# The products of the spectra behind the next row maxima in VectorE's order

## The chip, the cores and the metric

The kernel runs on one core of one Trainium2 chip. The core has five engines that run side by side, each through its own list of instructions in order: TensorE (PE, matrix products; its weight loads are shown apart as PEld), VectorE (DVE), ScalarE (ACT), GpSimd (POOL) and SyncE (SP, which here issues transfers). TensorE writes its results into PSUM, a small memory that VectorE and ScalarE read. The metric is the time of one execution on the device, in microseconds (us).

## The reference

The input `A_u` (1 x 2048 x 448) goes through two branches, and a gate per row mixes their outputs. Branch a is a state-space layer: a convolution along the 2048 rows, by way of a Fourier transform, with a filter made from the parameters. Branch b is attention with a memory: 16 heads of width 28 over 4 segments of 512 rows.

```python
def _A_ref(u, ...):
    K = 2.0 * jnp.einsum("dn,dnl->dl", C, P).real
    Kf = jnp.fft.rfft(K, L2)
    Uf = jnp.fft.rfft(u_t, L2)
    y = jnp.fft.irfft(Uf * Kf[None, :, :], L2)[:, :, :L]
...
def _B_ref(x, wq, wk, wv, wo, beta):
    for s in range(N):
        logits = jnp.einsum("bhqd,bhkd->bhqk", qs, ks) * scale + mask
        p = _softmax(logits, axis=-1)
        a_dot = jnp.einsum("bhqk,bhkd->bhqd", p, vs)
        ...
        o = g * a_mem + (1.0 - g) * a_dot
...
return g * a + (1 - g) * b
```

The product `Uf * Kf` is what the change touches. The row maximum that the softmax subtracts is what it is ordered against.

## The kernel before

The program has two halves. The first (about 425 us) makes the filter, the projections of the attention and the first step of the transform of `u`. The second half, `second_half`, weaves three streams of work into one order that is written out by hand. It loops over 16 blocks `i` (four segments of four groups of heads), and in each over six rounds `r`. One round takes one step of each stream:

- `weigh(i)`: three batches of matmuls `ps_w<-qu,ku` (the logits) and then one exponential on ScalarE, `PT<-ps_w`.
- `maxima(i + 2)`, two blocks ahead: first matmuls that lay the causal mask into a PSUM tile (`ps_mx<-mk`, "the masks" below), then the logits on top (`ps_mx<-ku,qu`), then one or two reductions on VectorE, `mx<-ps_mx` (a round with two covers 384 and 128 columns). `pair` interleaves these with the three batches of `weigh`: batch, masks, batch, logits and reduction, batch.
- `values(i - 1)`, in the first three rounds of a block: matmuls `ps_pv<-PT,V`.
- pieces of the end of a segment (`seg_end`): matmuls into `ps_m`, each read by one VectorE instruction that rescales a tile (`pvs`, `am`) or makes an output row block (`tb`).
- one step of `convolve`, in blocks 1 to 12. It works through 16 units `m`, which I count 1 to 16 in order of time. Its steps are, a round each: `transform(m)` (matmuls `ps_c<-gk,cf`, a copy `ks<-ps_c` by ScalarE and two transfers that swap halves of `ks`); `product(m - 1)` (matmuls `ps_c<-gu,cf`, then two VectorE multiplications `pr<-ps_c,ks`, "the products" below); an empty step; and `back(m - 1)` (matmuls `ps_c<-pr,cb`, in one round or two, then a copy `bs<-ps_c`).

The PSUM tiles `ps_w`, `ps_mx`, `ps_c`, `ps_m` and `ps_pv` exist once each. So the masks of a round wait for the reduction of the round before, `back` waits for both products, and a matmul into `ps_m` waits for the VectorE instruction that reads the last contents.

VectorE's instructions of this half go through `k.dve`, and each is pinned behind the one issued before it: the order of the Python calls is VectorE's order. `product` is called at the end of a round, so its two multiplications stand ahead of the reduction of the next round. All records of helpers carry the line of the helper: L1453 for VectorE and ScalarE here, L1499 for matmuls, L1502 for transposes.

## Time and profile before

| | us |
|---|---|
| runs, in rising order | 793.38, 797.98, 798.75 |
| median of the runs | 797.98 |
| the profiled execution | 792.33 |
| its span, first to last instruction | 790.5 |

The profiled execution is a fourth one, and its rows are what the prediction reads. Its stage of interest runs from about 477 to 705 us after the span's start: the stretch with the convolution's units 1 to 16. A row of the timeline gives start and duration in us, the engine, the line, the operation, the tiles (`out<-in`) with their shapes and how many instructions were merged into the row; in brackets stands how long the engine had been idle and what ended that. A weight load and a matmul are separate rows.

### The profile page before, as it was taken

How to read it: one execution, taken by the hardware profiler on the slowest of the kernel's cores; microseconds unless marked ns; L12 is line 12 of the kernel's file. 1: busy time of each engine (PE TensorE's matmuls, PEld its weight loads, DVE VectorE, ACT ScalarE, POOL GpSimd, SP SyncE). 2: the span in 40 equal slices, each digit the busy share in tenths (PEclk: the TensorE clock that was granted, in tenths of full speed). 3: DMA queues.
4: the chain of work that ended last, by engine and by line, in shares of the span. 5: the costliest groups of instructions: out<-in, count | busy, mean ns of one | idle time of the engine just before them, and what ended most of it. 6: DMA issues, size and time to landing. Idle time of an engine off the chain costs nothing.

```text
span 790.5 us, 19759 instructions
## 1 busy us (share of the span) xinstructions
PE 680.0 (86%) x8262; PEld 371.9 (47%) x8278; DVE 572.7 (72%) x768; ACT 493.8 (62%) x611; POOL 157.6 (20%) x193
## 2 busy tenths in 40 slices
PE   1695998999888998889996799889998899879997
PEld 1362565666555665556653443333443333334333
DVE  8989579878998798897976645655545755583486
ACT  4867689889998899998984225555434623451120
POOL 5304300111011101111020012414111411141110
PEclk9998999999999999999999979998998989999699
DMA  9338674135562345633457888997766875565875
GB/s 249 116 86 249 211 242 140 59 107 184 160 186 103 107 145 162 221 119 102 155 194 283 309 322 235 379 319 232 242 240 217 289 247 163 179 208 218 216 241 161
DMA packets 91550, 158.00 MB, mean 200 GB/s; under 512 B 22174, under 2 KB 59542, under 8 KB 91462
## 3 DMA queue, kind: packets, MB, share of 16 engines
q1 hardware_dynamic: 85530, 153.55, 59.4%
q10 hardware_dynamic: 5052, 2.33, 1.2%
q8 instruction: 65, 1.06, 0.6%
q0 software_dynamic: 880, 0.87, 0.3%
q14 instruction: 23, 0.19, 0.1%
HBM read 88.51 MB, written 60.24 MB: 188 GB/s over the span
## 4 chain that ended last, share of the span: by engine, by line
PE 54%; ACT 18%; DVE 14%; DMA 6%; issue 5%; SPq 2%; ACTq 0%; POOL 0%; DVEq 0%
PE ps_m L1499 22%; PE ps_c L1499 9%; ACT cs L1453 6%; PE ps_w L1499 5%; PE ps_mx L1499 5%; PE ps_pv L1499 5%; PE ps_k L1499 4%; PE ps_arg L1499 4%; DVE mx L1453 2%; DVE pr L1453 2%; DMA ku<-KD 2%; ACT EY L1453 2%; ACT L1453 1%; PE ps_m L1502 1%; DVE Y L413 1%
## 5 line engine op out<-in xcount | busy, mean ns | idle before, releaser
L1453 ACT ACTIVATE PT<-ps_w 128x1024 f32<-128x1024 f32 (+1 forms) x96 | 84.6, 881 | 145.1 <-PE ps_w L1499 139.2
L1453 DVE TENSOR_REDUCE mx<-ps_mx 128x2 f32<-128x1024 f32 (+3 forms) x128 | 102.4, 821 | 86.0 <-PE ps_mx L1499 83.7
L366 POOL TENSOR_TENSOR EX<-EX,cab 128x1024 f32<-128x1024 f32 x28 | 53.5, 1914 | 291.4 <-ACT EX L1453 269.0
L1453 ACT ACTIVATE cs<-ps_arg 128x1024 f32<-128x1024 f32 x97 | 94.5, 1024 | 8.6 <-DVE cs L386 6.2
L1499 PE MATMUL ps_w<-qu,ku 32*128 32x512 f32 (+3 forms) x768 | 94.7, 360 | 4.1 <-ACT PT L1453 4.0
L1094 POOL TENSOR_SCALAR_AFFINE_SELECT PT<-PT 128x256 f32<-128x256 f32 (+1 forms) x96 | 47.8, 498 | 241.8 <-ACT PT L1453 241.7
L1499 PEld LDWEIGHTS ps_w<-qu,ku 32*128 32x128 f32 x768 | 60.8, 195 | 70.5 <-ACT PT L1453 35.4
L1499 PE MATMUL ps_m<-xh,w 112*128 112x512 f32 x256 | 91.6, 410 | 0.2 <-DMA w<-WD 0.2
L1499 PE MATMUL ps_k<-Y,X 128*32 128x64 f32 x3584 | 63.8, 225 | 15.5 <-DVE Y L414 15.5
L409 DVE TENSOR_TENSOR X<-EX,cs 128x1024 f32<-128x1024 f32 x56 | 70.2, 1254 | 8.1 <-ACT cs L1453 7.5
L1499 PEld LDWEIGHTS ps_k<-Y,X 128*32 128x32 f32 x3584 | 54.5, 113 | 40.5 <-DVE Y L414 24.7
L413 DVE TENSOR_TENSOR Y<-EY,cs 128x1024 f32<-128x1024 f32 x56 | 68.2, 1218 | 0.0
L1453 ACT ACTIVATE cs<-cs 128x1024 f32<-128x1024 f32 x56 | 59.3, 1058 | 1.3
L1499 PEld LDWEIGHTS ps_m<-xh,w 112*128 112x128 f32 x256 | 48.0, 188 | 20.9 <-issue 10.0
L1453 ACT ACTIVATE EY<-ps_arg 128x1024 f32<-128x1024 f32 x52 | 52.1, 1040 | 5.3 <-PE ps_arg L1499 5.1
L1499 PE MATMUL ps_mx<-mk 32*128 32x128 bf16 (+5 forms) x768 | 36.4, 215 | 19.0 <-DVE mx L1453 19.0
L1499 PE MATMUL ps_m<-xl,w 112*128 112x512 f32 x128 | 50.2, 392 | 0.0
L1499 PE MATMUL ps_arg<-ct,lh 64*128 64x512 bf16 x224 | 45.1, 385 | 3.1 <-ACT EY L1453 1.6
L1499 PEld LDWEIGHTS <-lh 64*128 64x128 bf16 x392 | 20.4, 94 | 57.5 <-issue 45.8
L1499 PE MATMUL ps_mx<-ku,qu 32*128 32x512 f32 (+3 forms) x256 | 45.6, 389 | 1.4 <-DMA ku<-KD 1.4
L415 DVE SCALAR_TENSOR_TENSOR Y<-EY,cs 128x512 f32<-128x512 f32 x56 | 40.0, 714 | 8.7 <-ACT cs L1453 7.6
L1499 PE MATMUL ps_arg<-ce,lh 64*128 64x512 bf16 x168 | 33.7, 400 | 14.3 <-ACT EY L1453 7.2
(219 smaller groups left out, 1311.4 us busy)
## 6 DMA issues: line engine op xcount, KB each, us to landing
w<-WD SPq DMA_DIRECT2D x32, 448.0 KB
qu<-QD SPq DMA_DIRECT2D x16, 512.0 KB
ku<-KD SPq DMA_DIRECT2D x16, 512.0 KB
GU<-gs SPq DMA_DIRECT2D x32, 224.0 KB
GK<-gs SPq DMA_DIRECT2D x8, 896.0 KB
gk<-GK SPq DMA_DIRECT2D x16, 448.0 KB
gu<-GU SPq DMA_DIRECT2D x16, 448.0 KB
ks<-ks SPq DMA_DIRECT2D x32, 224.0 KB
```

Source lines behind the costliest of these rows:

```text
L366: nc.gpsimd.tensor_tensor(o, o, cab, ALU.mult)
L409: v.tensor_tensor(X, ex, t[:, :, 0], ALU.mult)
L413: v.tensor_tensor(Y[:, :, :, :32], lo, y[:, :, :, ::-1], ALU.mult)
L415: v.scalar_tensor_tensor(Y[:, 1, :, 32:], ey[:, :, 32:], -1.0, y[:, 1], ALU.mult, ALU.mult)
L1094: nc.gpsimd.affine_select(sl, sl, pat, ALU.is_ge, 0.0, base=0, channel_multiplier=-1)
L1453: x = op(*args, **kw)
L1499: tc.keep_in_program_order(nc.tensor.matmul(*args, **kw))
L1502: tc.keep_in_program_order(nc.tensor.transpose(*args))
```

## The change

`product` no longer issues its two multiplications. It puts them on a list `k.later`. `maxima` takes one from the list after the reductions of a step, and the round takes what is left after its pair of steps (and after `peak(behind)` in the first two rounds). `back` empties the list before it starts, in case something is still there.

```diff
         for b in range(2):
-            k.dve.tensor_tensor(pr[m][:, b], pt, x[:, b], ALU.mult)
+            k.later.append(functools.partial(k.dve.tensor_tensor, pr[m][:, b], pt, x[:, b], ALU.mult))
 
     def back(m):
 
+        k.catch_up()
         pt = k.ps("c")
...
                     mx[:, 2 * hp : 2 * hp + 2, 3 - t : 4 - t], pt[:, :, o : o + n], AX.X, ALU.max,
                 )
+            k.catch_up(1)
             yield
...
+    k.later = []
+
+    def catch_up(n=2):
+        for op in k.later[:n]:
+            op()
+        del k.later[:n]
+
+    k.catch_up = catch_up
...
                 peak(behind)
+            k.catch_up()
             if i > 0 and r < 3:
```

The order of instructions changes on VectorE alone. On TensorE, ScalarE, GpSimd and SyncE it is the same, instruction by instruction; no instruction is added or removed.

On VectorE, around unit 2's products, before (`x2` is two instructions; the numbers name buffers):

```order
L1453 TENSOR_REDUCE mx_6210<-ps_mx_6211 128x2
L1453 TENSOR_REDUCE mx_6210<-ps_mx_6253 128x2
L1453 TENSOR_TENSOR pr_6284<-ps_c_6279,ks_6047 128x896 x2
L1453 TENSOR_REDUCE mx_6210<-ps_mx_6296 128x2 x2
L1453 TENSOR_REDUCE mx_6210<-ps_mx_6334 128x2 x2
L1453 TENSOR_REDUCE mx_6210<-ps_mx_6373 128x2
```

The same stretch of VectorE's order after the change:

```order
L1464 TENSOR_REDUCE mx_6210<-ps_mx_6211 128x2
L1464 TENSOR_REDUCE mx_6210<-ps_mx_6253 128x2
L1464 TENSOR_REDUCE mx_6210<-ps_mx_6294 128x2 x2
L1464 TENSOR_TENSOR pr_6284<-ps_c_6279,ks_6047 128x896 x2
L1464 TENSOR_REDUCE mx_6210<-ps_mx_6334 128x2 x2
L1464 TENSOR_REDUCE mx_6210<-ps_mx_6373 128x2
```

Both products moved behind one round's reductions, here a round with two; no reduction stands between them.

On VectorE, around unit 16's products, before. `am` is a tile that is rescaled out of `ps_m` at the end of a segment:

```order
L1453 SCALAR_TENSOR_TENSOR am_8205<-am_8205,gh_1970,ps_m_8771 128x512
L1453 TENSOR_TENSOR pr_8779<-ps_c_8774,ks_8582 128x896 x2
L1453 TENSOR_REDUCE mx_8628<-ps_mx_8785 128x2
L1453 SCALAR_TENSOR_TENSOR am_8205<-am_8205,gh_1970,ps_m_8802 128x512
L1453 TENSOR_REDUCE mx_8628<-ps_mx_8811 128x2
```

And after:

```order
L1464 SCALAR_TENSOR_TENSOR am_8205<-am_8205,gh_1970,ps_m_8771 128x512
L1464 TENSOR_REDUCE mx_8626<-ps_mx_8783 128x2
L1464 TENSOR_TENSOR pr_8779<-ps_c_8774,ks_8582 128x896 x2
L1464 SCALAR_TENSOR_TENSOR am_8205<-am_8205,gh_1970,ps_m_8802 128x512
L1464 TENSOR_REDUCE mx_8626<-ps_mx_8811 128x2
```

Here too one reduction changed places with the two products; the rescaling of `am` stays behind all three.

## The prediction, made before the changed kernel ran

> **What bounds the kernel now.** I read the page's busy times first, then one window over the stage that the change touches, then the waits of its tiles, then the timeline at the 16 places where a unit's products run.

> ```profile
> PE 680.0 (86%) x8262; PEld 371.9 (47%) x8278; DVE 572.7 (72%) x768; ACT 493.8 (62%) x611; POOL 157.6 (20%) x193
> ```

> ```profile
> 477.00:705.00 228.00, 204.10 (x2368) 86.02 (x2371) 133.79 (x174) 106.24 (x143) 55.43 (x98) 0.94 0.73 244
> ```

> The second row is the table by windows for 477 to 705 us: length, then busy us and instructions of PE, PEld, DVE, ACT and POOL, then the granted clock, the share of the DMA engines and GB/s. TensorE is busy 204.1 of 228 us and VectorE 133.8. So TensorE sets the pace of this stage, and an edit on VectorE's order can only be worth the time that TensorE stands still because of VectorE. The next rows tell how much that is: from the view of the products, from the chain of waits in that window, and from the view of `mx` in it (who waited: us, times).

> ```profile
> L1453 DVE TENSOR_TENSOR pr<-ps_c,ks x32: 1078/1082/1092, 483.4 to 694.6; 128x896 f32<-128x896 f32 x32
> ```

> ```profile
> by line: PE ps_c L1499 24.6%; PE ps_m L1499 10.6%; PE ps_mx L1499 9.0%; PE ps_pv L1499 8.7%; issue 7.7%; DVE pr L1453 7.3%; PE ps_w L1499 7.2%; DVE mx L1453 6.0%; DMA ku<-KD 3.1%; ACT bs L1453 2.8%; ACT ks L1453 2.4%; DMA xt<-in_A_u 1.8%; A
> ```

> ```profile
> who waited for it (us, times):
>   PE ps_mx L1499: 13.6, 15
> ```

> The products are 32 instructions of 1.08 us, two to a unit. They and the reductions lie on the chain (7.3% and 6.0% of the window), which says that a reduction queued behind a pair of products is what TensorE's masks wait for. That wait is 13.6 us in all, in 15 of the 16 units. It is the most that the change can take away directly: 1.7% of the time.

> **The change, part by part.** Nothing is added or removed. Each unit's products change places with one round's reduction. So two things move: the reduction comes earlier, and the products come later, by the reduction and by the idle time until its input is there. What waits for the reduction gains; what waits for the products, or stands behind them on VectorE, may lose. The units fall into three kinds by what comes next.

> *First kind: nothing near waits for the products.* Unit 4, from the timeline:

> ```profile
> 518.31 0.36 PE L1499 MATMUL ps_mx<-ku,qu 32*128 32x256 f32 x2
> 518.33 2.09 DVE L1453 TENSOR_TENSOR pr<-ps_c,ks 128x896 f32<-128x896 f32 x2 [0.86 <-PE ps_c L1499]
> ...
> 520.34 0.68 DVE L1453 TENSOR_REDUCE mx<-ps_mx 128x2 f32<-128x512 f32 x1
> 521.07 0.23 PE L1499 MATMUL ps_mx<-mk 32*128 32x128 bf16 x2 [1.12 <-DVE mx L1453]
> ...
> 521.77 1.23 DVE L1453 TENSOR_REDUCE mx<-ps_mx 128x2 f32<-128x1024 f32 x1 [0.75 <-PE ps_mx L1499]
> ...
> 522.76 1.73 PE L1499 MATMUL ps_c<-pr,cb 64*64 64x448 f32 x16
> ```

> The reduction's input is complete at 518.31 + 0.36 = 518.67, but it runs at 520.34, behind the products. Put first (0.1 us after its input, an estimate from such rows), it runs from 518.77 to 519.45, and the products from 519.45 to 521.54. The masks were ready at 521.07 - 1.12 = 519.95, so their wait of 1.12 is gone. What is late next? The next reduction's input comes at 521.77 - 1.12 = 520.65 and has to wait for the products until 521.54, still earlier than before. `back` comes at 522.76 - 1.12 = 521.64, just behind the products. The whole 1.12 is kept. The other four of this kind (units 3, 8, 13 and 15) have these mask waits; in each the matmuls of `back` come 1.7 us or more after the masks, as in unit 4 (522.76 against 521.07), and no VectorE instruction that reads `ps_m` and is soon waited for stands behind the products:

> ```profile
> 508.70 0.23 PE L1499 MATMUL ps_mx<-mk 32*128 32x128 bf16 x2 [0.70 <-DVE mx L1453]
> ...
> 577.51 0.23 PE L1499 MATMUL ps_mx<-mk 32*128 32x128 bf16 x2 [0.19 <-DVE mx L1453]
> ...
> 654.38 0.23 PE L1499 MATMUL ps_mx<-mk 32*128 32x128 bf16 x2 [0.46 <-DVE mx L1453]
> ...
> 684.10 0.29 PE L1499 MATMUL ps_mx<-mk 32*128 32x128 bf16 x2 [1.18 <-DVE mx L1453]
> ```

> Sum of the first kind: 1.12 + 0.70 + 0.19 + 0.46 + 1.18 = 3.65 us gained.

> *Second kind: `back` follows at once* (units 1, 2, 5, 6, 9, 10). Unit 2, with unit 1's and unit 10's masks as first and last of the six:

> ```profile
> 486.77 0.23 PE L1499 MATMUL ps_mx<-mk 32*128 32x128 bf16 x2 [0.96 <-DVE mx L1453]
> ...
> 495.39 2.09 DVE L1453 TENSOR_TENSOR pr<-ps_c,ks 128x896 f32<-128x896 f32 x2 [0.97 <-PE ps_c L1499]
> ...
> 495.76 0.22 PE L1499 MATMUL ps_mx<-ku,qu 32*128 32x128 f32 x2
> ...
> 497.40 1.28 DVE L1453 TENSOR_REDUCE mx<-ps_mx 128x2 f32<-128x768 f32 x2
> ...
> 498.73 0.28 PE L1499 MATMUL ps_mx<-mk 32*128 32x256 bf16 x2 [0.83 <-DVE mx L1453]
> ...
> 499.47 1.73 PE L1499 MATMUL ps_c<-pr,cb 64*64 64x448 f32 x16
> ...
> 610.32 0.28 PE L1499 MATMUL ps_mx<-mk 32*128 32x256 bf16 x2 [0.84 <-DVE mx L1453]
> ```

> The input is there at 495.98; reductions 496.08 to 497.36, products to 499.45. The masks' 0.83 is gone, so `back` would come at 499.47 - 0.83 = 498.64, but now it waits for the products until about 499.49. Nothing is gained: the wait has moved from the masks to `back`. Where `back` follows its masks even closer the sign turns. Unit 1's `back` stands 0.46 behind its masks, at

> ```profile
> 487.23 0.98 PE L1499 MATMUL ps_c<-pr,cb 64*64 64x448 f32 x8
> ```

> and its products, which began at 483.4 (the row on `pr` above), end by unit 2's steps (0.59 to the input, 0.1, 1.28, 2.09) at 487.46: 0.23 lost. I put the six at nothing, between 6 x -0.23 = -1.4 and +1.5 (about a quarter of a us each, which those with the longest gap to `back` could keep).

> *Third kind: a VectorE instruction that empties `ps_m` stands behind the products* (units 7, 11, 12, 14, 16). Unit 16:

> ```profile
> 693.57 0.36 PE L1499 MATMUL ps_mx<-ku,qu 32*128 32x256 f32 x2
> 693.60 2.08 DVE L1453 TENSOR_TENSOR pr<-ps_c,ks 128x896 f32<-128x896 f32 x2
> ...
> 695.60 0.68 DVE L1453 TENSOR_REDUCE mx<-ps_mx 128x2 f32<-128x512 f32 x1
> 696.20 0.74 DVE L1453 SCALAR_TENSOR_TENSOR am<-am,gh,ps_m 128x512 f32<-128x512 f32 x1
> 696.34 0.23 PE L1499 MATMUL ps_mx<-mk 32*128 32x128 bf16 x2 [1.24 <-DVE mx L1453]
> ...
> 696.99 0.18 PEld L1499 LDWEIGHTS ps_m<-r,sel 8*128 8x128 f32 x1 [0.32 <-DVE am L1453]
> ```

> The input is there at 693.93; reduction 694.03 to 694.71, products to 696.79, `am` to 697.53. The masks' 1.24 is gone, but the next matmul into `ps_m`, which began at 696.99 when `am` had ended at 696.94, now begins at 697.58: 0.6 lost. Unit 12 goes the other way, since VectorE reaches the place late and the reduction's input is waiting:

> ```profile
> 632.27 2.08 DVE L1453 TENSOR_TENSOR pr<-ps_c,ks 128x896 f32<-128x896 f32 x2
> ...
> 634.27 0.68 DVE L1453 TENSOR_REDUCE mx<-ps_mx 128x2 f32<-128x512 f32 x1
> 634.86 0.73 DVE L1453 SCALAR_TENSOR_TENSOR pvs<-pvs,omg,ps_m 128x512 f32<-128x512 f32 x1
> 635.00 0.23 PE L1499 MATMUL ps_mx<-mk 32*128 32x128 bf16 x2 [1.86 <-DVE mx L1453]
> ...
> 636.99 0.79 PE L1499 MATMUL ps_m<-r,sel 8*128 8x512 f32 x1
> ```

> Reduction 632.27 to 632.95, products to 635.03, `pvs` to 635.76. The matmul into `ps_m` goes from 636.99 not to 635.13 but to 635.82: 1.17 gained. For units 7, 11 and 14 I take -0.2 each, nearer to unit 16 (there too a matmul into `ps_m` is near), with -0.6 each as the low end and the rest of the 13.6 us (13.6 - 3.65 - 5.4 for the second kind - 3.10 here, 1.4 together) as the high end. Sum of the third kind: -0.6 + 1.17 - 0.6 = 0.0.

> **The sum** is 3.65 + 0 + 0.0 = 3.6 us gained, 0.5%. Its ends: 3.65 - 1.4 - 1.2 = 1.0 and 3.65 + 1.5 + 2.0 = 7.1 (the third kind is -0.6 + 1.17 - 1.8 at the low end, -0.6 + 1.17 + 1.4 at the high one). That TensorE runs earlier has no second cost that I see: the queues of SyncE and GpSimd are unchanged and none of their transfers waits for the products.

> [...] The row: unit 4's reduction had its input at 518.67 and still began at 520.34, behind products that had begun first. [...] If a ready instruction could pass a waiting one, the products would lose nothing and the whole 13.6 us would be the gain.

> **Rivals.** *The whole wait goes*: the products end in time everywhere. For it: VectorE is idle 94 of 228 us. Against it: unit 2's and unit 16's rows. Gain 13.6.
> *Nothing comes of it*: what the masks gain is given back within two rounds, at `back` or at `ps_m`, also in the first kind. For it: unit 4's `back` clears the products by only 0.1 us. Gain 0.
> *Slower*: the products, now about 0.65 us later (the input's 0.6 us plus 0.1, in which VectorE has nothing it may start), delay the next round's reduction, and the masks of the round after wait for that as well, so the wait is longer and not shorter. Price: 16 x 0.65 = 10.4 us. It decides where the next reduction's masks follow its input by less than the products' overhang, 0.9 us in unit 4 (521.54 against 520.65). Against it: in unit 4 the 1.73 us of `back` stand between.

> **How the numbers follow.** The profiled execution took 792.33, its span 790.5; 3.6 less is 788.7. But it is the fastest of the four known: their mean is 795.6 and the median of the three runs 797.98. I start from 796.8, between these two. Forecast (gain 1.0 to 7.1): 796.8 - 3.6 = 793.2, chance 0.55. Nothing: 796.8, chance 0.26. The whole wait: 783.2, chance 0.09. Slower: 807.2, chance 0.10. The range 786 to 800 takes in the first two with the spread of the runs (5.4 us from end to end) and leaves out the last two, 0.19. About 1% (8 us) is what a measurement of this kernel can tell from no change. Faster by over 1% takes the whole-wait rival and the forecast's upper end, 0.16; slower by over 1% the last rival, 0.10; within 1% is the rest, 0.74.

> **What would show it.** In the profile of the changed kernel the masks' wait for `mx` should fall from 13.6 us to under 3. A new wait of `ps_c` for `pr` of about 3 us should appear in the units of the second kind, and the waits of `ps_m` for `am` and `pvs` should grow. The idle time of VectorE ahead of the reductions, put down to `ps_mx`, should grow by about 0.6 us a unit. The prediction is wrong if the masks still wait after the move, if `back` never waits for the products, or if the stage from unit 1 to unit 16 is not 1 to 7 us shorter.

## The result, and the profile after

| | before | after |
|---|---|---|
| median of the runs, us | 798.35 (6 runs, 793.38 to 802.75) | 787.12 (6 runs, 782.33 to 795.49) |
| profiled execution, us | 792.33 | 787.18 |
| its span, us | 790.5 | 785.5 |
| stage with the 16 units, us | 225.8 | 219.2 |

The ratio is 0.989, with a 95% interval from 0.985 to 0.994; it compares fast runs alone, so the slowest run of the changed kernel, 795.49, is not in it. In a second comparison the same two kernels gave 0.986 (0.981 to 0.991). By these ratios the change is worth 8.5 to 11 us. The time of 787.12 is in the range that was forecast, and the gain is two to three times the 3.6 us of the sum. The stage in the table runs from the end of the exponential of block 1, round 0 to that of block 13, round 0. Of the profiled pair, it shows 6.6 us of gain; the first half of the program, whose order is the same, differs by 4 us the other way (it ended 477.0 and 481.1 us after the start), and what follows the stage is 2.5 us shorter.

Where did the time in the stage come from? First the view of `mx` in the changed kernel, who waited for it, and the waits of that stage (who waited for whom: us, times, longest):

```profile
who waited for it (us, times):
...
  PE ps_mx L1510: 1.9, 2
```

```profile
PEld ps_c L1510 <- DVE pr L1464: 10.0, 9, 1.6
...
PE ps_c L1510 <- DVE pr L1464: 6.5, 6, 1.4
```

The masks' wait fell from 13.6 to 1.9 us, and `back`'s matmuls now wait 6.5 us for the products (the PEld row is the same waits, seen at the weight load). The rows at unit 4, in the timeline of the changed kernel:

```profile
522.07 0.98 PE L1510 MATMUL ps_c<-gu,cf 64*64 64x448 f32 x8 [0.41 <-ACT ks L1464]
...
523.15 0.36 PE L1510 MATMUL ps_mx<-ku,qu 32*128 32x256 f32 x2
...
523.56 0.69 DVE L1464 TENSOR_REDUCE mx<-ps_mx 128x2 f32<-128x512 f32 x1 [1.25 <-PE ps_mx L1510]
524.17 2.08 DVE L1464 TENSOR_TENSOR pr<-ps_c,ks 128x896 f32<-128x896 f32 x2
...
524.30 0.32 PE L1510 MATMUL ps_mx<-mk 32*128 32x128 bf16 x8
...
526.30 1.73 PE L1510 MATMUL ps_c<-pr,cb 64*64 64x448 f32 x16
```

The reduction begins 0.05 us behind its input (I had put 0.1), the masks no longer wait, and `back` follows the products at once. Unit 2, in the same view:

```profile
501.94 1.29 DVE L1464 TENSOR_REDUCE mx<-ps_mx 128x2 f32<-128x768 f32 x2 [1.64 <-PE ps_mx L1510]
...
503.14 2.08 DVE L1464 TENSOR_TENSOR pr<-ps_c,ks 128x896 f32<-128x896 f32 x2
...
505.28 1.74 PE L1510 MATMUL ps_c<-pr,cb 64*64 64x448 f32 x16 [0.93 <-DVE pr L1464]
```

Here the wait of 0.83 at the masks has become one of 0.93 at `back`, as the prediction worked it out. And unit 16:

```profile
692.10 2.08 DVE L1464 TENSOR_TENSOR pr<-ps_c,ks 128x896 f32<-128x896 f32 x2
...
694.10 0.74 DVE L1464 SCALAR_TENSOR_TENSOR am<-am,gh,ps_m 128x512 f32<-128x512 f32 x1
...
694.89 0.50 PE L1510 MATMUL ps_m<-r,sel 8*128 8x512 f32 x1 [2.04 <-DVE am L1464]
```

The matmul into `ps_m` waits 2.04 us for `am`, behind the products, where the masks waited 1.24 before.

Added up over the stage, TensorE waits no less for VectorE than before. Before, it was 13.6 us, all at the masks. After, it is 6.5 at `back`, 1.9 at the masks and 6.4 at `ps_m` (2.04, 1.89, 1.61 and 0.89): 15 us. (3.6 of these stand in unit 11, behind a transfer that the changed kernel reaches too early; more on that below.) So the waits alone do not explain the gain. The rows of the stage in the table by windows, before and after, name what else is different:

```profile
477.00:702.80 225.80, 202.02 (x2341) 85.17 (x2343) 131.91 (x172) 105.08 (x140) 54.96 (x96) 0.94 0.73 245
```

```profile
481.10:700.30 219.20, 192.28 (x2346) 81.46 (x2342) 130.57 (x172) 105.05 (x140) 55.00 (x96) 0.97 0.75 253
```

The granted clock is 0.97 where it was 0.94, and TensorE is busy 192 us with the same matmuls that took 202 before. In these two profiles the clock is granted in two steps, full and half (1.00 and 0.50). In the profile of before, half clock stood at these stretches of the stage; the columns are PE, PEld, DVE, ACT and POOL busy, then the clock:

```profile
533.90:537.30 3.40, 3.40 (x32) 1.32 (x32) 1.48 (x3) 1.20 (x2) 0.64 (x1) 0.51 0.87 303
547.60:551.00 3.40, 3.40 (x25) 0.95 (x17) 1.94 (x3) 1.02 (x1) 1.74 (x3) 0.50 0.14 46
595.40:602.20 6.80, 6.80 (x66) 2.87 (x69) 1.85 (x3) 2.11 (x3) 1.27 (x2) 0.50 0.32 123
636.30:643.10 6.80, 6.80 (x46) 2.26 (x42) 3.52 (x5) 2.02 (x3) 0.41 (x1) 0.50 0.72 260
684.10:687.50 3.40, 3.40 (x27) 1.15 (x30) 1.23 (x1) 1.17 (x2) 0.90 (x2) 0.50 0.35 142
697.80:701.20 3.40, 3.40 (x30) 1.37 (x24) 1.35 (x4) 0.77 (x1) 0.45 (x1) 0.50 0.01 2
```

27.3 us in six stretches, each 3.4 us or twice that. Each begins within 1.5 us behind a place where the masks had waited for a reduction: at 533.46, 546.98, 595.34, 635.00, 684.10 and 696.34 (waits of 0.95, 0.85, 0.96, 1.86, 1.18 and 1.24). The changed kernel's profile has four such stretches of 3.4 us, 13.7 us in all, each within 2 us of one of its own waits of TensorE: one for the products (1.39), one for a mask on GpSimd (1.64), and the two longest for `am` (1.89, inside which the stretch begins, and 2.04):

```profile
491.60:495.00 3.40, 3.40 (x28) 1.28 (x32) 1.20 (x2) 0.60 (x1) 0.03 (x1) 0.50 0.83 180
542.80:546.20 3.40, 3.40 (x20) 0.36 (x17) 1.79 (x4) 0.00 (x0) 0.00 (x0) 0.50 0.80 301
624.70:628.10 3.40, 3.13 (x17) 0.60 (x17) 1.35 (x2) 1.38 (x3) 2.13 (x3) 0.50 0.38 106
696.40:699.80 3.40, 3.40 (x28) 1.09 (x24) 1.67 (x4) 1.46 (x2) 0.00 (x0) 0.50 0.10 36
```

No wait of TensorE in the stage was as long as the shortest of these stretches: 1.86 us at most before and 2.04 after, against 3.4. Half clock stands here behind waits much shorter than itself.

```profile
680.70:684.10 3.40, 2.04 (x18) 0.45 (x13) 3.22 (x3) 1.02 (x1) 0.41 (x1) 1.00 0.77 278
```

```profile
689.80:693.20 3.40, 2.23 (x29) 0.78 (x30) 2.58 (x3) 1.17 (x2) 0.26 (x2) 1.00 0.79 282
```

TensorE is busy 0.60 of the first and 0.66 of the second. In the stages of the profiles of before and of the changed kernel, 117 such windows lie whole and ran at full clock (57 and 60). The five in which TensorE was busy least, 0.22 to 0.52 of the time, were all followed by half clock; of the eleven from 0.59 to 0.66, five; of the other 101, with 0.67 or more, none. So in these two profiles half clock went with the idle time within one window. That the same wait counts or not by where the window's borders fall is my reading of unit 15; no run here moved these borders on purpose.

### The profile page after: what moved, and what is told of

Same layout as the page of the kernel before. It is cut to its first block, busy times and chain, and to the rows that moved or that the text cites. A ratio compares the mean times of both kernels' runs of the same rounds, so it can differ in the third digit from the quotient of the medians.

```text
span 785.5 us, 19773 instructions
## 1 busy us (share of the span) xinstructions
PE 670.5 (85%) x8278; PEld 367.1 (47%) x8278; DVE 569.0 (72%) x768; ACT 493.8 (63%) x611; POOL 158.4 (20%) x193
## 4 chain that ended last, share of the span: by engine, by line
PE 52%; ACT 20%; DVE 13%; DMA 8%; issue 5%; SPq 1%; POOL 0%; ACTq 0%; DVEq 0%
PE ps_m L1510 21%; PE ps_c L1510 7%; ACT cs L1464 6%; PE ps_w L1510 5%; PE ps_pv L1510 4%; PE ps_arg L1510 4%; PE ps_k L1510 4%; PE ps_mx L1510 4%; DVE pr L1464 3%; DVE mx L1464 2%; ACT EY L1464 2%; ACT L1464 1%; DMA WD<-wsp 1%; PE ps_m L1513 1%; ACT PT L1464 1%
## 5 line engine op out<-in xcount | busy, mean ns | idle before, releaser
L1510 PE MATMUL ps_w<-qu,ku 32*128 32x512 f32 (+3 forms) x768 | 87.3, 344 | 5.4 <-ACT PT L1464 5.2
L1510 PEld LDWEIGHTS ps_w<-qu,ku 32*128 32x128 f32 x768 | 57.6, 186 | 69.0 <-ACT PT L1464 30.6
L409 DVE TENSOR_TENSOR X<-EX,cs 128x1024 f32<-128x1024 f32 x56 | 68.3, 1219 | 9.9 <-ACT cs L1464 9.2
L413 DVE TENSOR_TENSOR Y<-EY,cs 128x1024 f32<-128x1024 f32 x56 | 70.0, 1250 | 0.0
L1510 PEld LDWEIGHTS ps_m<-xh,w 112*128 112x128 f32 x256 | 48.8, 190 | 21.4 <-issue 10.4
L1510 PE MATMUL ps_pv<-PT,V 128*32 128x128 f32 (+3 forms) x512 | 45.8, 456 | 2.1 <-POOL PT L1096 1.6
L1510 PE MATMUL ps_m<-wo,pvs 128*128 128x448 f32 x96 | 43.0, 579 | 1.5 <-ACT mn L1464 1.1
```

The lines of the kernel that those rows point to most:

```text
L409: v.tensor_tensor(X, ex, t[:, :, 0], ALU.mult)
L413: v.tensor_tensor(Y[:, :, :, :32], lo, y[:, :, :, ::-1], ALU.mult)
L1510: tc.keep_in_program_order(nc.tensor.matmul(*args, **kw))
```

## The experiments

Two theories. **A**: the gain is the time in which TensorE no longer stands still, the prediction's reason. **B**: TensorE stands still about as long, but at places that bring fewer stretches of half clock. A third, **C**, came with a control: any more work for TensorE keeps the clock up.

All were timed beside the kernel before on the same chip. "Clock" is the mean granted clock over all runs of a kernel; the next two columns are from its one profile.

| kernel | median us | ratio to before, interval | clock | stage us | half clock in it, us |
|---|---|---|---|---|---|
| before (45 runs beside the later kernels; the prediction's profile) | 797.5 | | 0.945 | 225.8 | 27.3 |
| before_again | 797.14 | 1.000 (0.996 to 1.005) | 0.943 | 229.2 | 34.1 |
| the changed kernel | 787.12 | 0.989 (0.985 to 0.994) | 0.960 | 219.2 | 13.7 |
| after_again | 785.72 | 0.986 (0.981 to 0.991) | 0.961 | 222.2 | 23.9 |
| late_roomy | 785.74 | 0.983 (0.977 to 0.989) | 0.960 | 218.2 | 13.7 |
| late_tight | 794.03 | 0.997 (0.993 to 1.001) | 0.949 | 225.6 | 27.3 |
| before_filled | 790.08 | 0.990 (0.985 to 0.995) | 0.960 | 220.4 | 6.8 |
| filled_elsewhere | 807.16 | 1.011 (1.006 to 1.016) | 0.952 | 236.4 | 20.5 |
| roomy_filled | 787.77 | 0.986 (0.981 to 0.990) | 0.961 | 217.9 | 6.8 |
| late_held | 782.32 | 0.979 (0.974 to 0.984) | 0.959 | 214.9 | 17.1 |
| late_held_2 | 781.50 | 0.982 (0.977 to 0.986) | 0.959 | 217.2 | 20.5 |
| late_held_filled | 783.56 | 0.981 (0.975 to 0.986) | 0.957 | 214.1 | 10.2 |
| split_tight | 780.27 | 0.979 (0.974 to 0.984) | 0.953 | 208.8 | 10.2 |
| split_all | 778.33 | 0.977 (0.972 to 0.982) | 0.964 | 210.4 | 10.2 |

**The two kernels again.** No edit.

> The kernel before once more, for a second profile of it. Theory B: the masks' waits are the same 13 to 14 us, since they follow from the order; the half clock in the stage is again 20 us or more, most of it beginning within 4 us behind a wait of the masks, though not in the same units as in the first profile. Theory A says nothing of where half clock falls.

> The changed kernel once more, to see how much of its gain is the same from run to run. Theory A (TensorE stands still for less time) and theory B (TensorE stands still about as long, but fewer stretches of half clock follow) both expect 0.985 to 0.994 of before. They differ in the profile: A expects the sum of TensorE's waits for VectorE in the stage at 7 us or less and any amount of half clock; B expects that sum near the 13.6 us of before, and under 17 us of half clock in the stage against 27 us in the profile of before.

Theory B's expectation of before held: 14.3 us of masks' waits, 34.1 us of half clock in seven stretches, each beginning within 2.5 us of a masks' wait, and five of them in units that had one in the first profile too. The changed kernel's second profile again has 16.0 us of waits for VectorE, so A's limit of 7 us is refuted. Its half clock was 23.9 us, more than the 17 that B allowed: how many stretches fall is not the same from run to run, though the waits nearly are. The mean clock over all runs, 0.960 and 0.961 against 0.945 and 0.943, is the steadier witness.

**Which units carry the gain.** `late_roomy` moves six units' products, as in this diff; `late_tight` has the other ten in the list, (1, 2, 5, 6, 7, 9, 10, 11, 14, 16):

```diff
-            k.later.append(functools.partial(k.dve.tensor_tensor, pr[m][:, b], pt, x[:, b], ALU.mult))
+            if m + 1 in (3, 4, 8, 12, 13, 15):
+                k.later.append(functools.partial(k.dve.tensor_tensor, pr[m][:, b], pt, x[:, b], ALU.mult))
+            else:
+                k.dve.tensor_tensor(pr[m][:, b], pt, x[:, b], ALU.mult)
```

> Products behind the maxima in units 3, 4, 8, 12, 13 and 15 alone, ahead of them in the other ten. Theory A: these are the units that keep their gain, so 4 to 5 us, 0.994 to 0.995 of before, no wait of the back transform for the products. Theory B: ten waits of the masks of 0.6 to 1.2 us remain, each of which can bring a stretch of half clock, so half of the gain of the whole change or less, 0.994 to 1.0.

> The rest: products behind the maxima in units 1, 2, 5, 6, 7, 9, 10, 11, 14 and 16 alone. Theory A: waits of the back transform and of ps_m take the place of the masks' waits, 0.998 to 1.003 of before. Theory B: the same waits remain at another place, so half clock as before, 0.998 to 1.003; if the place of the wait matters for the clock, down to 0.993.

The six units alone give all of the gain, 0.983, and the other ten give 0.997, nothing that can be told from before. The split by kinds was right (the six are the first kind and unit 12). But `late_roomy` gained more than either theory allowed it: the ten remaining waits of the masks (10.3 us) brought only 13.7 us of half clock in its profile.

**Work in the waits.** `before_filled` is the kernel before, with matmuls on constants where TensorE is about to wait; they write a tile that is overwritten at once. `filled_elsewhere` has the same matmuls two rounds later (`k.rounds = 4`). The kernel before already runs matmuls on constants (`ps_pv<-wz`) in rounds with little other work; these come on top:

```diff
     def product(m):
...
+        k.rounds = 2
...
         for b, hp in STEPS:
             pt = k.ps("w")
+            k.rounds -= 1
+            if k.rounds == 0:
+                for _ in range(4):
+                    k.mm(pt[:, 0], k.wz[:, :128], k.wz, start=True, stop=True)
```

> The kernel before, with four matmuls on constants (into ps_w, overwritten at once) at the start of the round whose masks wait for the reduction: TensorE still waits there as long, but does something in that time. Theory A: nothing gained, 1.000 to 1.003 of before, since the masks still come only when the reduction has ended. Theory B: the stretches of half clock behind these places go away; with 27 us at half clock in the stage before, up to 13 us, so 0.985 to 0.994 of before, and under 14 us of half clock in the stage.

> The control to before_filled: the kernel before with the same 64 matmuls on constants, but two rounds later, where TensorE is not about to wait for a reduction. They cost 16 times 4 matmuls of 0.21 us, 13 us of TensorE time at full clock. If the clock is kept up by work in the waits (theory B), the waits and the half clock stay as before, and time is added: 1.003 to 1.017 of before, mean granted clock of the runs 0.94 to 0.95. If any added matmuls keep the clock up (rival C: what counts is TensorE's work per stretch of the program, wherever it stands), the clock rises to 0.955 or more, and the time is 0.995 to 1.005.

This pair decides between A and B. In `before_filled` the order on VectorE is that of before, and the masks come no sooner: they are only busy-waited for. Unit 9, before:

```profile
595.34 0.29 PE L1499 MATMUL ps_mx<-mk 32*128 32x128 bf16 x2 [0.96 <-DVE mx L1453]
...
596.12 1.77 PE L1499 MATMUL ps_c<-pr,cb 64*64 64x448 f32 x8
```

and with the filling, in its timeline:

```profile
595.02 1.02 PE L1505 MATMUL ps_w<-wz 128*128 128x512 bf16 x4 [0.36 <-ACT PT L1459]
595.02 1.28 DVE L1459 TENSOR_REDUCE mx<-ps_mx 128x2 f32<-128x768 f32 x2
...
596.36 0.23 PE L1505 MATMUL ps_mx<-mk 32*128 32x128 bf16 x2
...
596.82 0.98 PE L1505 MATMUL ps_c<-pr,cb 64*64 64x448 f32 x8
```

The masks begin when the reduction ends in both. But the eight matmuls of `back` take 0.98 us and not 1.77: before, half clock (0.50) stood there from 595.4 on, and with the filling the only half clock of the stage is at 618.6 to 625.4. The kernel is 0.990 of before, as much as the change itself gave in the first comparison, with the same mean clock of 0.960. The control, with the same work elsewhere, kept the masks' waits (16.0 us) and was 9 us slower than before. Its clock rose a little, from 0.945 to 0.952, just beyond what B had allowed, so C has a part in it, less than half of what work in the waits does. The half clock in the stage goes the same way: 6.8 us with work in the waits and 20.5 with the work elsewhere, against 27.3 and 34.1 in the profiles of before.

**More filling.** `roomy_filled` and `late_held_filled` add the four matmuls where masks still wait:

> late_roomy and the filling together: products behind the maxima in the six units, and in the other ten, where the masks still wait, four matmuls on constants in the wait. Theory B: the ten waits of late_roomy, 10.3 us in its profile, no longer bring half clock, so another 2 to 5 us, 0.977 to 0.984 of before, mean clock 0.965 or more. Theory A: the filling is worth nothing, 0.983 to 0.986 as late_roomy.

> late_held with the four matmuls on constants in the wait of the masks in the seven units that are left. Theory B: 0.975 to 0.981 of before, mean clock 0.965 or more, the best so far. Theory A: as late_held.

A miss for theory B as I had put it. The half clock in the stage did fall (13.7 to 6.8, and 17.1 and 20.5 to 10.2), but the stage became only 0.3 us shorter than `late_roomy`'s and 0.8 and 3.1 shorter than `late_held`'s two, and the times did not move beyond their intervals. Part of it is unit 14, whose masks wait in no profile of before: filling there cost 0.87 us (its four rounds took 13.51 us in all three kernels with filling in the waits, 12.64 without). Also, in these three profiles what follows the stage took 89.0 to 89.5 us, against 84.7 to 87.9 in the others. Half clock goes with that: 17.1 to 17.2 us of it there, against 10.5 to 14.3 in the others but the two of before (17.7). Nothing in the edit is placed there, and what sets that amount I have not found.

**`ps_m` first.** `late_held` also moves units 7, 11 and 16, but takes their products from the list only after the round's piece of `seg_end`, so behind `am` or `pvs`:

```diff
+        k.held = m + 1 in (7, 11, 16)
...
-            k.catch_up(1)
+            if not k.held:
+                k.catch_up(1)
...
                 busy = busy or x == "po"
+            k.catch_up()
```

> late_roomy with units 7, 11 and 16 moved as well, but with the instruction that empties ps_m ahead of the products (order: reduction, am or pvs, products). If the waits of ps_m in those units came from the products standing ahead of am and pvs, they are gone (under 1 us of waits for am and pvs in the profile), and the masks' wait falls from 10.3 to about 7.6 us: 1 to 3 us better than late_roomy, 0.979 to 0.983 of before. Where only the length of TensorE's waits counts (theory A), 2.7 us better.

> late_held once more, beside the two versions below on the same chip: 0.974 to 0.985 of before.

Unit 7's four rounds took 11.62 us, against 12.74 before and 12.97 in the changed kernel. Over the whole, 0.979 and 0.982 against `late_roomy`'s 0.983: in the direction expected, with intervals that overlap. The profiles bear out the reason in part: TensorE's waits for `am` and `pvs` fell to 0.4 and 1.1 us and those of the masks to 4.8 and 5.5, but `back` now waits 2.4 us for the products, which the expectation had not counted.

**One product ahead, one behind.** `split_tight` does it in the seven units that `late_held` left alone, as in this diff; in `split_all`, where the condition is `if b:` alone, it is done in all:

```diff
-            if m + 1 in (3, 4, 7, 8, 11, 12, 13, 15, 16):
+            if b or m + 1 in (3, 4, 7, 8, 11, 12, 13, 15, 16):
```

> late_held, and in the other seven units (1, 2, 5, 6, 9, 10, 14) the first product ahead of the reduction and the second behind it. In those units the reduction's input comes 0.6 us after the products could start, so one product (1.04 us) ahead delays the reduction by 0.4 to 0.5 us and not by 1.5, and the second product ends 0.65 us earlier than with both behind. By unit 2's rows the masks then wait for nothing and the back transform for 0.2 us at most: 0.6 to 0.7 us in each of six units, about 4 us at full clock, and fewer stretches of half clock. 0.970 to 0.978 of before; masks' wait under 2 us and back transform's wait under 2 us in the profile.

> One product ahead and one behind the reduction in all 16 units. In the nine units that late_held moved whole, the reduction now comes up to 0.5 us later, where the masks had 0.1 to 0.5 us to spare: 0 to 2 us worse than split_tight, 0.971 to 0.980 of before.

Unit 2 in the timeline of `split_all`:

```profile
496.49 1.09 DVE L1473 TENSOR_TENSOR pr<-ps_c,ks 128x896 f32<-128x896 f32 x1 [0.97 <-PE ps_c L1519]
...
497.50 1.28 DVE L1473 TENSOR_REDUCE mx<-ps_mx 128x2 f32<-128x768 f32 x2
...
498.70 1.08 DVE L1473 TENSOR_TENSOR pr<-ps_c,ks 128x896 f32<-128x896 f32 x1
498.83 0.28 PE L1519 MATMUL ps_mx<-mk 32*128 32x256 bf16 x2
...
499.83 1.73 PE L1519 MATMUL ps_c<-pr,cb 64*64 64x448 f32 x16 [0.18 <-DVE pr L1473]
```

The first product fills the time in which the reduction's input is still being made, and both waits are nearly gone. Over the stage the masks' and `back`'s waits came to 0.2 and 2.6 us in `split_tight`, and 1.6 and 2.1 in `split_all`; under 2 each had been expected for the first. The time of `split_tight`, 0.979, is just outside its 0.970 to 0.978. `split_all` has the lowest median of the study, 0.977 (0.972 to 0.982), 19 us below the median of before beside it and some 8 us below the changed kernel. That it would be slower than `split_tight` did not show; the two cannot be told apart.

## Why the prediction was right in kind and too small

**Which waits go, and what takes their place: right.** A stretch of four rounds around each unit (from one exponential's end to the fourth after it) repeats from kernel to kernel to 0.02 us where no half clock falls into it, with few exceptions. So each unit's own gain can be measured without the clock, with products ahead from one profile and behind from another, both free of half clock there:

| unit | products ahead, us | products behind, us | gain measured | gain forecast |
|---|---|---|---|---|
| 3 | 10.76 (before) | 9.79 (after) | 0.97 | 0.70 |
| 4 | 10.31 (before) | 9.01 (after) | 1.30 | 1.12 |
| 8 | 16.55 (before) | 16.05 (after) | 0.50 | 0.19 |
| 13 | 14.15 (before) | 14.01 (after) | 0.14 | 0.46 |
| 15 | 11.10 (before_again) | 9.66 (after) | 1.44 | 1.18 |
| 1 | 9.64 (before) | 9.85 (late_tight) | -0.21 | -0.23 |
| 2 | 10.98 (before) | 10.92 (after) | 0.06 | 0 |
| 5 | 9.64 (late_roomy) | 9.85 (after) | -0.21 | 0 |
| 9 | 10.73 (late_roomy) | 10.93 (after) | -0.20 | 0 |
| 10 | 11.28 (before) | 10.93 (after_again) | 0.35 | 0 |
| 7 | 12.74 (before) | 12.97 (after) | -0.23 | -0.2 |
| 14 | 12.65 (before) | 12.65 (after) | 0.00 | -0.2 |

The first kind sums to 4.35 us, forecast 3.65. The five of the second kind sum to -0.2, forecast nothing; unit 10 is among the exceptions, with 11.39 us in `after`. Unit 7 cost 0.23 as said, through `ps_m`. Units 6, 11, 12 and 16 had half clock in every profile of the one order or the other, and are not in the table. For unit 12 the kernel with filling can stand in: 11.46 us in `before_filled` and 10.42 in `after`, a gain of 1.0 where 1.17 was forecast.

**The order on VectorE: right.** The sums took it that the reduction, put first, holds the products until its input has come. No row that the prediction read shows that, since in unit 4's the products were ready first; unit 4 of the changed kernel does. The products' input was complete at 523.05 and VectorE idle, yet it began the reduction first, at 523.56 behind its input of 523.51, and the products at 524.17. The sum by that order, about 4 us, fits the units; the 13.6 us that products passing the waiting reduction would have brought was not there.

**The signs.** The masks' wait fell under 3 us in the first profile (1.9) and to 3.1 in the second. `back`'s new wait was 6.5 and 7.0 us where about 3 was expected, and VectorE's idle time put down to `ps_mx` rose from 69.1 to 74.4 us, about 0.3 a unit and not 0.6. The stage became 6.6 and 6.9 us shorter, at the upper end of the 1 to 7.

**The step that failed: "an edit on VectorE's order can only be worth the time that TensorE stands still because of VectorE".** The gain of the change stayed under the 13.6 us drawn from it, but `split_all`, also an edit on VectorE's order alone, gained about 19. The same matmuls kept TensorE busy for less time: 192.6 us in the stage of `split_all`, 192.3 in that of the changed kernel, 202.0 before. The prediction quoted the granted clock of the stage, 0.94, and gave it no term and no rival. What a stretch costs can be read from the same four rounds with and without one: unit 5, products ahead, 10.81 and 9.64; unit 15, 12.57 and 11.10; unit 9 with 6.8 us of half clock, 13.68 and 10.73. That is 1.2 to 1.5 us for each 3.4 us. Between the two profiles of before (30.7 us of half clock on the mean) and of after (18.8), 11.9 us or three and a half stretches are gone: 4 to 5 us on top of the waits. With the waits' 4 us that makes 8 to 9; the stage's own difference between those pairs of profiles is 6.8 (227.5 and 220.7 on the mean). Part of the rest stands in unit 11, where the changed kernel came too early for a transfer: its four rounds took 15.26 us and 17.79 in its two profiles, 11.28 in the first of before, with half clock and with VectorE waiting 2.5 and 4.1 us for `dn<-pvs`. Over the stage VectorE waited 5.2 and 5.9 us for that transfer, and none and 0.8 before. So "That TensorE runs earlier has no second cost that I see" failed too, in the other direction.

**What was luck.** The sum with its ends, 1.0 to 7.1 us, missed the gain of 8.5 to 11. The time is in the range because the range was widened for the spread of the runs. And faster by over 1%, where both measured ratios lie, had the chance 0.16.

**The tail.** The rest of the gain is behind the stage, where the order is the same: 87.7 and 87.8 us before, 85.2 and 85.5 after, with 17.7 us of half clock in both profiles of before and 10.6 and 10.5 in those of after. Most of it is one stretch, 13.7 us long in both profiles of before (735.3 to 749.0 in the first) and 6.8 in both of after. What sets its length stays open; `late_held`, in two profiles of one kernel, had 84.9 us with 10.7 of half clock and 87.7 with 14.3.

**The rivals.** "The whole wait goes" had the time nearest to the measured one (783.2 against 787.1; the forecast had 793.2), but not the reason: the sum of TensorE's waits did not fall. "Nothing comes of it" is outside both intervals, and the first kind kept its gain. "Slower" did not come: the next reductions were held back to the end of the products, as in unit 4, where `back` covered it.

## What to carry to other kernels

When an engine that feeds TensorE is reordered, add up TensorE's waits before and after, and beside them the granted clock: here a wait of about a microsecond that half clock followed cost as much again behind it (1.2 to 1.5 us for each 3.4 us of half clock). Look for it in windows of the length at which the clock changes, 3.41 us here. If a wait can't be removed, try work on constants in it: here it was worth as much as the better order (0.990 against 0.989 of before), though only in the wait (1.011 elsewhere); on top of the better orders it gave nothing that could be told. And where two instructions must be placed around one whose input is late, the gap before that input is the place for the first of them.

## What the runs showed that I had not expected

Waits of TensorE of 0.8 to 2.0 us, with matmuls on both sides, were followed by 3.4 us at half clock or a multiple of it (six of the 15 waits of the masks in one profile of before, seven in the other), while others of the same length were not (0.96 and 1.12 us in units 1 and 4). What went with half clock in the two profiles that were cut into windows of 3.41 us was how much of one window TensorE was busy: at 0.52 or less half clock followed in all five, from 0.59 to 0.66 in five of eleven, at 0.67 or more in none of 101. A stretch cost 1.2 to 1.5 us of the program's time. The number of stretches in one and the same kernel differs from run to run (13.7 and 23.9 us in the stage for the changed one). Over the 45 runs of before the mean clock was 0.945, and the times ran from 791 to 809 us.
